# A new order of all pieces in a fused attention and channel-mix kernel: loads of late batches ahead of use, stores and DMA transposes between them

## The chip, the cores and the metric

The kernel runs on one NeuronCore of a Trainium2 chip. The metric is the device time of one execution in microseconds (us). A profile, taken by the hardware profiler, gives a span that is about 2 us shorter than that time.

Names: PE is the tensor engine, DVE the vector engine, ACT the scalar engine, POOL the engine whose queue issues the loads, SP the queue that issues stores and DMA transposes. A wait of an engine is idle time before an instruction, named by what ended it.

## The reference

Inputs q, k, v are [8 batches, 8 heads, 576, 64] in float32. Linear attention with an RMS norm is followed by a channel mix with weights 512x1024 (w_k), 1024x512 (w_v) and 512x512 (w_r):

```python
def _attn_ref(q, k, v, g_norm):
    kv = np.einsum('bhsd,bhse->bhde', k, v)
    out = np.einsum('bhsd,bhde->bhse', q, kv)
    rms = np.sqrt(np.mean(out * out, axis=-1, keepdims=True) + 1e-06)
    return (out / rms * g_norm).astype(np.float32)

def _moe_ref(x, mu_k, mu_r, w_k, w_v, w_r):
    x_prev = np.concatenate([np.zeros((B, 1, D), dtype=np.float32), x[:, :-1, :]], axis=1)
    xk = mu_k * x + (1.0 - mu_k) * x_prev
    xr = mu_r * x + (1.0 - mu_r) * x_prev
    k = np.maximum(xk @ w_k, 0.0)
    v = k * k @ w_v
    r = 1.0 / (1.0 + np.exp(-(xr @ w_r)))
    return (r * v).astype(np.float32)
```

## The kernel before

The kernel is a list of named pieces and one long string, ORDER, that gives the order in which they are emitted. Each engine runs its own pieces in that order. A token is `name:engine:slots`; a slot is a buffer of a small set. The pieces that matter here, by batch b and group g of 512 rows:

- `load_k4.0` loads k of batch 4 (float32 in DRAM, written as bf16), on the POOL queue. There are two slots each for k, v and q.
- `kv4.0` multiplies k by v of batch 4 on PE. It is the last reader of their slots.
- `qTd4` transposes q of batch 4 by DMA on the SP queue (batches 3 to 7; batches 0 to 2 are transposed by PE, `qT2.0`). `u4.*` then multiplies by kv.
- `K`, `R`, `V` are the matmuls with w_k, w_r and w_v, `S` the stores on the SP queue.

How the order is run, and a load (cut):

```python
    def run(self, order, idle):
        held = {}
        for token in order.split():
            name, eng, slots = (token.split(":") + ["", ""])[:3]
            if name == "idle":
                idle(int(eng), int(slots))      # matmuls on zeros
                continue
            p = self.pieces[name]
            ...
            for b, s in zip(new, slots):
                old = held.get((b.tag, s))
                assert old is None or all(u.done for u in old.users), name
                b.slot = int(s)
                held[(b.tag, s)] = b
            p.done = True
            p.fn(self.ENG[eng] if eng else next(iter(p.on)))
...
    BUFS = {
        "k": (2, (NP, H, NJ * HD), BF16),
        "v": (2, (NP, H, NJ * HD), BF16),
        "q": (2, (NP, H, NJ * HD), BF16),
        "qT": (2, (128, H, NI * NP), BF16),
        ...
        "out": (4, (128, 2, C), FP32),
        "ps": (4, (128, 2, 512), FP32),
    }
...
    def load(b, n, h0, h1):
        def fn(_):
            nc.gpsimd.dma_start(out=get(kvq[(n, b)])[:, h0:h1, :], in_=rows(n, b, h0, h1))
...
            def q_dma(_):
                nc.sync.dma_start_transpose(out=get(qT).rearrange(...), in_=get(qin).rearrange(...))
...
    def idle(n, slot):
        for _ in range(n):
            nc.tensor.matmul(tiles[("ps", slot)][:, 0, HS:512], zeros[:, 0:128], zeros[:, HS:512], start=True, stop=True)
```

The part of ORDER that decides the loads of batches 3 to 5 (all other tokens cut):

```
kv2.0::2 ... load_q3.0::1 ... load_v3.0::1 ... load_q4.0::0 load_k3.0::1 ... kv3.0::2 ... qTd3::1 ...
load_v5.0::0 load_v4.0::1 ... load_k4.0::0 ... S0.2 qTd4::0 ... load_k5.0::1 ... kv4.0::2 ... load_v6.0::1 ...
kv5.0::0 ... load_k6.0::0 ... S0.1 S0.3 S1.1 ... load_q5.0::1 ... S1.3 ... kv6.0::0 ... S1.0 S0.0 qTd5::1
```

Note that v5 takes slot 0, which kv2 frees, and v4 the slot that kv3 frees. k4 could go out after kv2, but stands behind v5 and v4 in the one POOL queue.

## Time and profile before

| | before |
|---|---|
| median time at the start, 3 runs | 220.16 us (220.15 to 221.36) |
| span of the profiled run | 219.1 us |
| PE busy | 193.7 us (88%) |
| longest wait of PE | 11.0 us, for k of batch 4 |
| last matmul ends, after the start | 213.2 us |

The page first. Each digit is the busy share, in tenths, of one of 40 equal slices of the span (5.5 us each); PEclk is the clock granted to PE in tenths of full speed.

```profile
...
PE   7758999999899009999999999999999999999990
...
PEclk9999999999999956999999999999999999999997
DMA  6999999999999995999999840100004606001184
...
```

PE is full nearly everywhere but in the slices from 71 to 82 us. DMA is full up to about 130 us, and the clock drops just after PE's gap.

Busy time of the engines in stretches of 10 us; the number after the engines is the granted clock, then the share of time that the DMA engines were busy (it sums the time of all packets, so it can pass 1) and what they moved:

```profile
...
core 0: us, PE busy (x) PEld busy (x) DVE busy (x) ACT busy (x) POOL busy (x), PEclk, DMA share, GB/s
...
10.00:20.00 10.00, 6.07 (x71) 3.00 (x70) 9.43 (x26) 8.68 (x15) 5.54 (x9) 1.00 1.27 203
...
70.00:80.00 10.00, 1.06 (x12) 0.24 (x9) 4.11 (x7) 2.58 (x4) 0.00 (x0) 0.80 1.23 253
80.00:90.00 10.00, 7.91 (x72) 3.96 (x72) 1.87 (x4) 3.19 (x3) 3.06 (x4) 0.69 0.81 130
...
```

PE works 1.06 us of 70-80, and at 0.69 of its clock in 80-90.

PE's own timeline there (start, duration, what, and in brackets the idle time before it and what ended that):

```profile
...
70.62 0.44 PE L432 MATMUL ps<-qT,kv 64*64 64x288 bf16 x8
82.09 1.49 PE L349 MATMUL ps<-v,k 96*64 96x64 bf16 x48 [11.03 <-DMA k<-in_k_dram]
83.51 3.23 PE L600 MATMUL ps<-xk,w_k 128*128 128x512 bf16 x8
86.58 3.62 PE L622 MATMUL ps<-w_r,xr 128*128 128x512 bf16 x16
...
```

kv4 (the 48 matmuls with k) waits 11.03 us for k4. The eight w_k matmuls behind it (L600) take 3.23 us, against 1.90 at 68.79 us in the same view.

The loads on POOL, with what each waited for, and the SP queue (an SP row's length is how long issuing kept the queue):

```profile
...
43.07 0.77 POOL L277 DMA_DIRECT2D q<-in_q_dram  x1 [10.07 <-PE ps L407]
43.83 0.77 POOL L277 DMA_DIRECT2D k<-in_k_dram  x1
45.86 0.77 POOL L277 DMA_DIRECT2D v<-in_v_dram  x1 [1.26 <-PE ps L349]
60.05 0.77 POOL L277 DMA_DIRECT2D v<-in_v_dram  x1 [13.42 <-PE ps L349]
60.81 1.58 POOL L277 DMA_DIRECT2D k<-in_k_dram  x2
...
```

```profile
...
47.32 8.04 SPq L390 DMA_TRANSPOSE qT<-q  x1
...
57.27 6.62 SPq L390 DMA_TRANSPOSE qT<-q  x1
63.94 13.38 SPq L582 DMA_DIRECT2D out_dram<-out  x12
```

In ORDER's sequence these are q4, k3, v5, then v4 at 60.05 and k4, k5 at 60.81. Twelve store DMAs follow at 63.94. The time from issue to landing of v4 and k4:

```profile
...
v<-in_v_dram POOLq DMA_DIRECT2D x1, 576.0 KB, 15.6
k<-in_k_dram POOLq DMA_DIRECT2D x1, 576.0 KB, 21.2
...
```

k4 takes 21.2 us, so it lands at 82.0, when PE starts kv4.

### The profile page before, as it was taken

To read this page: it belongs to the slowest core of one execution; us is meant where nothing else is said; L and a number is where in the kernel's file an instruction comes from. 1 tells how busy PE (TensorE), PEld (TensorE's weight loads), DVE (VectorE), ACT (ScalarE), POOL (GpSimd) and SP (SyncE) were. 2 spreads that over 40 slices of the span, in tenths; PEclk is the share of its full clock that TensorE was granted. 3 is DMA by queue.
4 is the path that set the end of the run, shared out by engine and by line. 5 is a ranking of instruction groups with operands and counts; after the bars stand their busy time and mean duration, and the time that the engine had idled before them with its cause. 6 is when DMAs were issued, how large, how long until landed. Compare 5 with 4: busy or idle time off the path is not lost.

```text
span 219.1 us, 3799 instructions
## 1 busy us (share of the span) xinstructions
PE 193.7 (88%) x1526; PEld 94.1 (43%) x1526; DVE 138.9 (63%) x254; ACT 125.1 (57%) x152; POOL 28.8 (13%) x45
## 2 busy tenths in 40 slices
PE   7758999999899009999999999999999999999990
PEld 6424453543443005534444764444444444444450
DVE  1499068975996501688989898829934992422260
ACT  2579674789365301977669778367566444481100
POOL 7954420120030005000400000000000000000000
PEclk9999999999999956999999999999999999999997
DMA  6999999999999995999999840100004606001184
GB/s 151 192 202 206 202 206 204 204 204 195 163 156 98 265 246 63 202 204 150 163 237 188 220 129 3 48 0 3 0 0 114 174 3 193 0 0 48 31 223 131
DMA packets 39301, 29.71 MB, mean 136 GB/s; under 512 B 13548, under 2 KB 34804, under 8 KB 39284
## 3 DMA queue, kind: packets, MB, share of 16 engines
q0 software_dynamic: 21232, 16.48, 50.1%
q1 hardware_dynamic: 17348, 12.03, 26.2%
q10 hardware_dynamic: 704, 0.95, 1.4%
q8 instruction: 12, 0.20, 0.4%
q14 instruction: 5, 0.04, 0.0%
HBM read 33.56 MB, written 9.44 MB: 196 GB/s over the span
## 4 chain that ended last, share of the span: by engine, by line
PE 64%; DMA 21%; DVE 6%; POOL 4%; issue 1%; ACT 1%; DVEq 0%; POOLq 0%
PE ps L656 24%; PE ps L600 22%; DMA k<-in_k_dram 17%; PE ps L622 10%; DMA v<-in_v_dram 5%; PE ps L349 2%; POOL q L277 1%; DVE xT L536 1%; PE ps L432 1%; POOL v L277 1%; PE ps L531 1%; POOL k L277 1%; DVE sqk L607 1%; DVE sq L195 1%; PE ps L515 1%
## 5 line engine op out<-in xcount | busy, mean ns | idle before, releaser
L656 PE MATMUL ps<-w_v,sqk 128*128 128x512 bf16 (+1 forms) x296 | 67.1, 374 | 0.3 <-DMA w_v<-in_moe_w_v_dram 0.3
L600 PE MATMUL ps<-xk,w_k 128*128 128x512 bf16 (+1 forms) x320 | 66.9, 363 | 0.0
L604 ACT ACTIVATE relu<-ps 128x1024 bf16<-128x1024 f32 x36 | 36.4, 1023 | 41.4 <-PE ps L600 37.1
L600 PEld LDWEIGHTS <-w_k 128*128 128x128 bf16 x320 | 30.9, 99 | 32.0 <-issue 2.8
L656 PEld LDWEIGHTS <-sqk 128*128 128x128 bf16 x296 | 27.5, 98 | 32.2 <-issue 1.4
L607 DVE TENSOR_TENSOR sqk<-relu 128x1024 bf16<-128x1024 bf16 x36 | 24.1, 687 | 26.3 <-ACT relu L604 26.2
L622 PE MATMUL ps<-w_r,xr 128*128 128x512 bf16 x144 | 34.4, 379 | 0.1
L660 DVE TENSOR_TENSOR out<-ps,sig 128x1024 f32<-128x1024 f32 (+2 forms) x21 | 22.2, 1068 | 14.2 <-issue 6.8
L627 ACT ACTIVATE sig<-ps 128x1024 bf16<-128x1024 f32 x18 | 18.4, 1022 | 13.1 <-PE ps L622 6.6
L536 DVE TENSOR_TENSOR xT<-uT,ps 128x576 bf16<-128x576 bf16 x28 | 20.0, 750 | 8.0 <-PE ps L531 8.0
L187 ACT ACTIVATE t<-d,mu_sb 128x576 bf16<-128x576 bf16 x29 | 20.7, 767 | 5.9 <-DVE d L557 5.8
L622 PEld LDWEIGHTS <-xr 128*128 128x128 bf16 x144 | 13.5, 98 | 15.9 <-DVE xr L567 0.8
L349 PE MATMUL ps<-v,k 96*64 96x64 bf16 x288 | 6.2, 204 | 11.9 <-DMA k<-in_k_dram 11.8
L181 ACT CAST uT<-ps 128x576 bf16<-128x576 f32 x16 | 9.9, 639 | 6.9 <-PE ps L432 6.5
L277 POOL DMA_DIRECT2D q<-in_q_dram x12 | 8.6, 715 | 36.5 <-DMA qT<-q 17.1
L277 POOL DMA_DIRECT2D v<-in_v_dram x11 | 8.0, 729 | 38.3 <-PE ps L349 36.9
L557 DVE TENSOR_TENSOR d<-xT 128x1152 bf16<-128x1152 bf16 (+1 forms) x18 | 12.5, 692 | 0.6
L183 DVE CAST uT<-ps 128x576 bf16<-128x576 f32 x12 | 8.9, 754 | 5.5 <-PE ps L432 5.4
L567 DVE TENSOR_TENSOR xr<-t,xT 128x1152 bf16<-128x1152 bf16 (+1 forms) x18 | 12.1, 686 | 0.2
L189 DVE TENSOR_SCALAR t<-d,mu_sb 128x576 bf16<-128x576 bf16 x35 | 11.8, 377 | 0.2
L567 DVE TENSOR_TENSOR xk<-t,xT 128x1152 bf16<-128x1152 bf16 (+1 forms) x18 | 11.7, 683 | 0.1
L349 PEld LDWEIGHTS <-k 96*64 96x64 bf16 x288 | 5.6, 120 | 13.7 <-DMA k<-in_k_dram 12.3
(60 smaller groups left out, 127.1 us busy)
## 6 DMA issues: line engine op xcount, KB each, us to landing
out_dram<-out SPq DMA_DIRECT2D x22, 192.0 KB
q<-in_q_dram POOLq DMA_DIRECT2D x6, 576.0 KB, 12.2
k<-in_k_dram POOLq DMA_DIRECT2D x6, 576.0 KB, 15.5
v<-in_v_dram POOLq DMA_DIRECT2D x6, 576.0 KB, 16.2
out_dram<-out SPq DMA_DIRECT2D x22, 128.0 KB
out_dram<-out SPq DMA_DIRECT2D x22, 64.0 KB
w_k<-in_moe_w_k_dram POOLq DMA_DIRECT2D x2, 512.0 KB, 12.7
w_v<-in_moe_w_v_dram POOLq DMA_DIRECT2D x2, 512.0 KB, 15.2
```

Source lines behind the costliest of these rows:

```text
L187: nc.scalar.mul(out=dst, in_=src, mul=by)
L277: nc.gpsimd.dma_start(out=get(kvq[(n, b)])[:, h0:h1, :], in_=rows(n, b, h0, h1))
L349: nc.tensor.matmul(get(pkv)[64 * e:64 * e + 64, 0, HD * i:HD * i + HD], get(kin)[:, h, HD * j:HD * j + HD], get(vin)[:, h, HD * j:HD * j + ...
L536: nc.vector.tensor_tensor(out=get(xT)[:, 2 * i:2 * i + 2, NP + c:NP + c + HS], in0=flat(slice(2 * i, 2 * i + 2))[:, :, c:c + HS], in1=get( ...
L567: nc.vector.tensor_tensor(out=dst[:, hsl, c0:c0 + S], in0=get(t[key])[:, hsl, :], in1=get(xT)[:, hsl, 0:S], op=ALU.add)
L600: nc.tensor.matmul(get(ps)[:, fc % 2, a0:a1], w_k_sb[:, cc, 128 * fc:128 * fc + 128], xk[:, cc, x0:x0 + a1 - a0], start=(cc == 0), stop=(c ...
L604: nc.scalar.activation(out=get(rt), in_=get(ps), func=AF.Relu)
L607: nc.vector.tensor_mul(out=get(sqk)[:, 2 * f2:2 * f2 + 2, :], in0=get(rt), in1=get(rt))
L622: nc.tensor.matmul(get(ps)[:, ci % 2, :], xr[:, cc, c:c + 128], w_r_sb[:, cc, :], start=(cc == 0), stop=(cc == NHP - 1))
L627: nc.scalar.activation(out=get(sg), in_=get(ps), func=AF.Sigmoid)
L656: nc.tensor.matmul(get(ps)[:, ci % 2, cs], get(sqk)[:, fc, 128 * ci:128 * ci + 128], w_v_sb[:, fc, cs], start=(fc == 0), stop=(fc == NFC - 1))
L660: nc.vector.tensor_mul(out=get(ot)[:, xs, cs], in0=get(ps)[:, xs, cs], in1=get(sg)[:, xs, cs])
```

## The change

Its intent: a new sequence of all pieces, with k, v and q of the late batches loaded well ahead of use, and stores and DMA transposes put between the loads. No piece is added, removed or altered; the engine that does a copy or a scaling changes for some. (`land` is a number for the planner that made the order; nothing reads it at run time.) The diff replaces all of ORDER; its core, with cuts:

```diff
 ORDER = """
-    early_k::0 zero cast_k:D:0 g_load sel_load early_v::1 mu_k_load:A mu_r_load:A cast_v:A:0 idle:28:0 kv0.0::0 load_v0.2
-    load_k0.2 load_q0.2::0 kv0.1::1 load_q0.0 load_q0.4 load_v0.4 load_k0.4 load_q0.6 ident qT0.1::2 qTc0.1:A:0 ones kvm0.1::0
+    zero mu_r_load:A early_k::0 mu_k_load:S early_v::1 cast_k:A:0 load_q1.0::0 load_q0.2::1 load_q0.0 load_q0.4 ident idle:28:0
+    qT1.0::0 ident9 cast_v:A:0 kv0.0::1 ones kvm0.0::0 qT0.1::2 qT0.0::3 g_load qTc1.0:A:0 load_k0.4 load_v0.4 load_k0.2
 ... (cut)
-    load_v3.0::1 sig1.0::0 uc2.3:A sq2.1:D load_q4.0::0 load_k3.0::1 K1.0::3 K1.6::0 relu1.1::1 st2::1 rs2::1 sqk1.1::1 K1.1
-    xk2.0 V1.0b tr2.2:D:0 kvc3.0.1:A tr2.0:A o1.1::0 load_v5.0::0 load_v4.0::1 V1.1a V1.1b o1.0::1 load_k4.0::0 K2.6::3 K2.7
-    K2.5::2 K2.4 S0.2 qTd4::0 relu2.3::1 u3.0::0 u3.2::1 uc3.2:A:1 relu2.2::0 load_k5.0::1 K2.2::3 K2.3 u3.1::1 uc3.0:D xr2.2
+    tr1.2:A:1 load_q4.0::1 xk1.2 xk1.0 o0.0::2 tr1.0:A K1.2::0 load_v3.0::1 K1.3 xr1.0 o0.1::3 xr1.2 relu1.1::1 load_k3.0::1
+    relu1.0::0 u2.1::2 K1.4::0 u2.0::3 uc2.0:A uc2.1:D sqk1.1 u2.2::2 sqk1.0 uc2.2:D sq2.1:D:0 sq2.0:A load_k4.0::0 K1.5
+    relu1.2::1 sqk1.2 R1.1::1 V1.1a::3 st2::2 rs2::1 R1.0 sp2.0::02 x2.0.1::0 x2.0.0 V1.0a V1.0b sp2.1::20 load_v4.0::0 x2.1.1
+    x2.1.0 d2.0::0 d2.2 sig1.0::2 S0.1 qTd3::0 load_q5.0::0 tk2.0:D:0 xk2.0 tk2.2:A xk2.2 R1.3::1 R1.2 V1.1b V1.3a::0 V1.2a
+    u3.3::3 sqk2.2 load_v5.0::1 load_k5.0::1 kv4.0::0 uc3.1:A K2.2::1 K2.3 uc3.3:D sq3.0:D:0 sq3.1:D relu2.3::0 st3::3 rs3::0
 ... (cut)
 """
-    p_wr = add("load_w_r", {"POOL": 0.75}, lambda _: load_w(w_r_sb, moe_w_r), land=2.5)
+    p_wr = add("load_w_r", {"POOL": 0.75}, lambda _: load_w(w_r_sb, moe_w_r), land=3.0)
```

v4 now takes slot 0, freed by kv2, and stands with k4 ahead of q5, v5 and k5.

More of the change, by code (lines that the diff above doesn't have):

```diff
@@ L15 @@
 ORDER = """
-    early_k::0 zero cast_k:D:0 g_load sel_load early_v::1 mu_k_load:A mu_r_load:A cast_v:A:0 idle:28:0 kv0.0::0 load_v0.2
-    load_k0.2 load_q0.2::0 kv0.1::1 load_q0.0 load_q0.4 load_v0.4 load_k0.4 load_q0.6 ident qT0.1::2 qTc0.1:A:0 ones kvm0.1::0
-    ident9 mu_mm::3 mu kvm0.0 load_k0.6 load_v0.6 qT0.0::1 u0.1::3 qTc0.0:A sq0.1::0 qT0.2::2 u0.0::0 uc0.1:D:0 ss0.1::1 sq0.0
-    qTc0.2:D uc0.0:D rs0.1::0 load_w_r kv0.2::3 kvm0.2 x0.1::0 ss0.0::2 d0.1::0 load_k1.0::1 load_v1.0::1 rs0.0::1 load_w_k0
@@ L20 @@
-    x0.0 u0.2::0 sq0.2 tk0.1:D:0 qT0.3::1 kv0.3::3 ss0.2::2 uc0.2:A rs0.2::0 d0.0 kvm0.3 load_w_k1 qTc0.3:D tk0.0:A x0.2
-    tr0.0:D:1 xr0.0 d0.2 tr0.1:D xr0.1 u0.3::0 sq0.3 ss0.3::3 uc0.3:A rs0.3::1 x0.3 d0.3 tr0.2:A tk0.2:A tr0.3:A R0.0::12 R0.1
-    load_k1.4 load_v1.4 load_q1.0::1 tk0.3:A xr0.2 kv1.0::0 xk0.0 xk0.1 xr0.3 R0.2 R0.3.1 R0.3.0 sig0.0::0 xk0.2 xk0.3 K0.3::3
-    kvm1.0::1 K0.2 K0.0::0 relu0.1::0 K0.1 relu0.0::1 sqk0.0::0 sqk0.1 load_q1.4 K0.6::1 K0.4::3 K0.5 K0.7 qT1.1::0 load_w_v0
@@ L24 @@
-    qTc1.1:D:1 sig0.1::1 relu0.2::1 kv1.2::2 qT1.0::3 qT1.3::0 relu0.3::0 qTc1.0:A qT1.2::1 kvm1.2 u1.1::2 uc1.1:A:1 qTc1.3:D
-    u1.0::3 u1.3::0 sel qTc1.2:D u1.2::1 V0.1a::2 uc1.0:D sq1.0:D:0 uc1.3:A uc1.2:A sq1.1:D st1::3 rs1::0 load_w_v1 sqk0.2
-    sqk0.3 load_q2.0::0 V0.0a sp1.1::01 load_k2.0::0 V0.1b x1.1.0::1 x1.1.1 sp1.0::30 x1.0.1 V0.0b V0.3a::1 x1.0.0 d1.2::0
-    qT2.3::0 qTc2.3:A:0 d1.0 tr1.0:D:1 xr1.0 tr1.2:A load_v2.0::0 xr1.2 qT2.2::3 V0.2a V0.3b qT2.1::0 qTc2.2:A qTc2.1:A V0.2b
@@ L28 @@
-    qT2.0::3 tk1.0:A:0 R1.2::0 R1.3 tk1.2:D o0.0::2 qTc2.0:D o0.1::3 xk1.0 xk1.2 kv2.0::2 sig1.1::2 R1.1::3 R1.0 load_q3.0::1
-    kvc2.0.2:A:0 kvc2.0.0:A kvc2.0.1:A u2.1::1 u2.2::0 uc2.2:A:0 uc2.1:D K1.3::2 u2.3::1 u2.0::0 uc2.0:D sq2.0:D:0 K1.2
-    load_v3.0::1 sig1.0::0 uc2.3:A sq2.1:D load_q4.0::0 load_k3.0::1 K1.0::3 K1.6::0 relu1.1::1 st2::1 rs2::1 sqk1.1::1 K1.1
-    relu1.0::0 K1.7 sqk1.0 relu1.3::1 K1.5::2 sp2.1::13 K1.4 x2.1.1::0 x2.1.0 sqk1.3 relu1.2::0 V1.2a::0 V1.3a sp2.0::31
-    kv3.0::2 sqk1.2 qTd3::1 x2.0.1 d2.2::0 x2.0.0 d2.0 tk2.2:A:1 kvc3.0.0:A:1 kvc3.0.2:A V1.2b V1.0a::1 V1.3b tk2.0:D xk2.2
@@ L33 @@
-    xk2.0 V1.0b tr2.2:D:0 kvc3.0.1:A tr2.0:A o1.1::0 load_v5.0::0 load_v4.0::1 V1.1a V1.1b o1.0::1 load_k4.0::0 K2.6::3 K2.7
-    K2.5::2 K2.4 S0.2 qTd4::0 relu2.3::1 u3.0::0 u3.2::1 uc3.2:A:1 relu2.2::0 load_k5.0::1 K2.2::3 K2.3 u3.1::1 uc3.0:D xr2.2
-    xr2.0 u3.3::0 kv4.0::2 uc3.1:A load_v6.0::1 K2.0::1 K2.1 sqk2.3::0 sqk2.2 uc3.3:A relu2.1::1 sq3.1:D:0 sq3.0:D relu2.0::0
-    R2.1::0 R2.0 sig2.0::1 R2.3::3 R2.2 sig2.1::2 sqk2.1 kvc4.0.2:D:0 kvc4.0.1:D sqk2.0 kvc4.0.0:D u4.3::1 uc4.3:D:0 u4.0::2
@@ L37 @@
-    kv5.0::0 kvc5.0.2:D:1 uc4.0:D st3::1 rs3::0 load_k6.0::0 V2.3a::3 V2.3b S0.1 S0.3 S1.1 sp3.0::21 kvc5.0.0:D kvc5.0.1:A
-    u4.2::0 x3.0.1::1 x3.0.0 V2.2a load_q5.0::1 uc4.2:A sq4.1:A:0 sp3.1::10 x3.1.0 V2.2b u4.1::2 x3.1.1 uc4.1:A S1.3 sq4.0:A
-    d3.0::0 V2.1a::1 V2.1b V2.0a tk3.0:A:1 d3.2 tk3.2:D xk3.2 load_q6.0::0 xk3.0 kv6.0::0 st4::2 S1.0 S0.0 qTd5::1 rs4::1 V2.0b
-    o2.0::3 tr3.0:A:0 kvc6.0.1:A:0 kvc6.0.2:D K3.5::2 K3.4 K3.7::1 K3.6 qTd6::0 o2.1::1 S2.0 S1.2 S2.2 load_q7.0::1 load_v7.0::0
@@ L41 @@
-    load_k7.0::1 relu3.2::1 kvc6.0.0:A sqk3.2::1 xr3.0 tr3.2:D xr3.2 relu3.3::0 sqk3.3 K3.1::2 K3.0 K3.2::3 K3.3 sp4.0::01
-    relu3.0::1 sqk3.0 x4.0.0::0 relu3.1::0 sqk3.1 x4.0.1 R3.0::2 R3.1 R3.2::0 sp4.1::31 x4.1.0 x4.1.1 d4.0::0 d4.2 R3.3
-    sig3.0::0 V3.0a::2 V3.0b sig3.1::1 u5.3::3 u5.1::1 u6.0::0 uc5.3:A:1 V3.1a uc6.0:A:0 uc5.1:D tk4.0:D:1 u5.2::3 u5.0::1
-    u6.1::0 V3.1b uc5.0:A sq5.0:A:0 uc5.2:D xk4.0 o3.0::2 tk4.2:D uc6.1:A sq5.1:A V3.2a::1 V3.2b V3.3a xk4.2 u6.2::3 u6.3::0
-    st5::2 uc6.2:D tr4.0:A:0 uc6.3:D rs5::0 V3.3b K4.2::3 K4.3 relu4.1::1 K4.7::0 K4.6 xr4.0 sp5.0::23 tr4.2:D o3.1::0 xr4.2
@@ L46 @@
-    qTd7::1 x5.0.1::1 S2.1 S3.0 x5.0.0 K4.0::1 K4.1 sp5.1::32 relu4.3::0 sqk4.3::0 x5.1.0 sqk4.1 K4.4::0 K4.5 relu4.0::0
-    sq6.1:A:0 relu4.2::1 x5.1.1 d5.2::0 sq6.0:D tk5.2:D:1 sqk4.0 R4.1::3 R4.0 R4.3::1 st6::2 kv7.0::0 R4.2 S3.1 S3.2 S2.3
-    tr5.2:A:0 rs6::1 xk5.2 d5.0 sqk4.2 tk5.0:D kvc7.0.2:D:1 kvc7.0.0:D xk5.0 sig4.1::2 kvc7.0.1:A sig4.0::0 V4.0a::2 V4.1a V4.1b
-    u7.3::1 u7.1::0 u7.2::3 V4.0b uc7.1:D:1 uc7.3:D K5.7::0 uc7.2:A o4.0::3 xr5.2 tr5.0:D xr5.0 K5.1::3 K5.6 relu5.3::0 K5.0
@@ L50 @@
-    relu5.0::1 sqk5.0::1 sqk5.3 K5.2::1 K5.3 K5.5::2 relu5.1::1 K5.4 R5.0::0 R5.1 sp6.0::31 relu5.2::0 sig5.0::1 x6.0.1::0
-    x6.0.0 sqk5.1 V4.2a::2 V4.3a sp6.1::10 u7.0::3 uc7.0:A sq7.1:A:0 sq7.0:A sqk5.2 x6.1.0 x6.1.1 d6.0::0 d6.2 tk6.0:A:1
-    tr6.2:A:0 V4.3b V5.3a::3 V5.1a::1 V4.2b V5.1b R5.3::0 V5.3b R5.2 V5.0a S3.3 tk6.2:D o4.1::2 xk6.2 xk6.0 sig5.1::0 K6.3::2
-    K6.2 V5.0b K6.7::0 K6.6 V5.2a V5.2b relu6.1::1 relu6.3::0 tr6.0:D xr6.2 xr6.0 sqk6.1::0 K6.0::2 sqk6.3 o5.1::1 o5.0::0 K6.1
@@ L54 @@
-    st7::0 K6.5::3 K6.4 rs7::0 relu6.0::1 R6.2::1 R6.3 sp7.1::02 relu6.2::0 sig6.1::2 sqk6.0 x7.1.0::1 x7.1.1 R6.0::3 R6.1
-    sp7.0::01 sqk6.2 x7.0.0 x7.0.1 d7.0::0 d7.2 S4.1 tk7.2:D:1 tk7.0:D tr7.0:A:0 sig6.0::0 V6.0a::2 V6.0b V6.3a::0 V6.1a V6.2a
-    V6.3b V6.1b xk7.2 S5.0 S5.2 S4.0 S5.1 V6.2b xk7.0 o6.0::3 K7.4::1 K7.5 K7.7::3 tr7.2:A o6.1::0 K8.4::2 K8.0::0 relu7.2::1
-    xr7.0 K8.1 relu8.0::0 sqk8.0::1 xr7.2 sqk7.2::0 S5.3 S4.2 S6.2 S6.0 S4.3 S6.1 K7.3::1 K7.2 K8.6::0 relu7.1::0 K8.7
-    relu8.3::1 sqk8.3 K8.5 relu8.2::1 sqk8.2 K7.6 sqk7.1 R8.3::1 K8.3::0 K8.2 relu8.1::1 relu7.3::0 sqk7.3 R8.2 K7.1::2
@@ L59 @@
-    sig8.1::1 sqk8.1 K7.0 relu7.0::0 R8.0::0 R8.1 sig8.0::0 V8.1a::3 V8.1b o8.0.1.0::1 sqk7.0 R7.3::1 R7.2 R7.0::2 sig7.1::2
-    V7.0a::0 V7.3a::3 V7.2a V7.3b V7.0b V7.2b o7.1::2 R7.1 V7.1a V7.1b S7.2 S7.3 S8.1.1.0:A S6.3 sig7.0::2 V8.0a::1 V8.0b
-    V8.2a::3 o7.0::3 S7.0 S7.1 o8.0.0.0 S8.0.0.0:S V8.2b o8.1.2.0::2 S8.2.2.0:A V8.3.0a::2 V8.3.0b V8.3.1a::0 o8.1.3.0
-    S8.3.3.0:S V8.3.1b o8.1.3.1 S8.3.3.1:A
+    zero mu_r_load:A early_k::0 mu_k_load:S early_v::1 cast_k:A:0 load_q1.0::0 load_q0.2::1 load_q0.0 load_q0.4 ident idle:28:0
@@ new lines @@
+    qT1.0::0 ident9 cast_v:A:0 kv0.0::1 ones kvm0.0::0 qT0.1::2 qT0.0::3 g_load qTc1.0:A:0 load_k0.4 load_v0.4 load_k0.2
+    qTc0.0:A:1 load_v0.2 qT0.2::1 mu_mm::0 u0.0::3 qTc0.2:A kv0.2::1 sq0.0::0 mu kvm0.2 qTc0.1:D ss0.0::0 uc0.0:D:0 rs0.0::0
+    load_q0.6 load_v0.6 load_k0.6 u0.2::1 kv0.1::2 kvm0.1 x0.0::0 d0.0::0 sq0.2 ss0.2::0 sel_load uc0.2:A qT0.3::3 u0.1::2
+    rs0.2::1 x0.2 qTc0.3:D d0.2 sq0.1 kv0.3::1 ss0.1::0 load_w_r uc0.1:A rs0.1::0 sel kvm0.3 qT1.1::3 tr0.2:A:0 u0.3::2 tr0.0:D
@@ new lines @@
+    load_v1.0::1 load_k1.0::1 x0.1 sq0.3 ss0.3::1 d0.1 xr0.2 xr0.0 uc0.3:A rs0.3::1 tr0.1:D xr0.1 R0.0::02 R0.1 x0.3 tk0.2:D:1
+    d0.3 qTc1.1:D tr0.3:D xr0.3 R0.2 R0.3.1 load_w_k0 kv1.0::1 tk0.3:A tk0.0:A tk0.1:D xk0.3 xk0.0 xk0.2 xk0.1 R0.3.0 load_w_k1
+    kvm1.0::1 K0.3::3 K0.2 K0.0::1 sig0.0::0 sig0.1::1 relu0.1::0 K0.4::0 u1.1::2 uc1.1:D:1 sqk0.1::0 K0.5 load_q1.4 load_v1.4
+    load_k1.4 relu0.2::1 K0.1 relu0.0::0 sqk0.0 u1.0::3 qT1.3::2 qT1.2::0 uc1.0:A sq1.0:A:0 kv1.2::1 K0.6::3 qTc1.2:D qTc1.3:D
@@ new lines @@
+    kvm1.2 u1.3::0 sqk0.2 u1.2::2 uc1.2:A load_q2.0::1 K0.7 load_w_v0 load_w_v1 load_v2.0::0 load_k2.0::0 load_q3.0::0 qT2.1::1
+    qT2.0::2 uc1.3:D sq1.1:D st1::0 qTc2.1:D:1 qTc2.0:D qT2.2::1 rs1::0 relu0.3::0 sp1.1::20 qTc2.2:D V0.3a::1 V0.1a::3
+    x1.1.1::1 x1.1.0 sqk0.3 sp1.0::02 x1.0.1 x1.0.0 V0.2a V0.0a d1.2::0 V0.1b V0.2b V0.0b V0.3b qT2.3::2 tk1.2:A:0 d1.0 tk1.0:D
+    tr1.2:A:1 load_q4.0::1 xk1.2 xk1.0 o0.0::2 tr1.0:A K1.2::0 load_v3.0::1 K1.3 xr1.0 o0.1::3 xr1.2 relu1.1::1 load_k3.0::1
@@ new lines @@
+    K1.7::3 K1.6 relu1.3::0 kv2.0::0 kvc2.0.1:A:0 kvc2.0.0:D K1.0::1 sqk1.3::1 qTc2.3:A K1.1 kvc2.0.2:A u2.3::3 uc2.3:A:0
+    relu1.0::0 u2.1::2 K1.4::0 u2.0::3 uc2.0:A uc2.1:D sqk1.1 u2.2::2 sqk1.0 uc2.2:D sq2.1:D:0 sq2.0:A load_k4.0::0 K1.5
+    relu1.2::1 sqk1.2 R1.1::1 V1.1a::3 st2::2 rs2::1 R1.0 sp2.0::02 x2.0.1::0 x2.0.0 V1.0a V1.0b sp2.1::20 load_v4.0::0 x2.1.1
+    x2.1.0 d2.0::0 d2.2 sig1.0::2 S0.1 qTd3::0 load_q5.0::0 tk2.0:D:0 xk2.0 tk2.2:A xk2.2 R1.3::1 R1.2 V1.1b V1.3a::0 V1.2a
+    V1.3b V1.2b sig1.1::0 tr2.2:A:1 tr2.0:D o1.0::0 qTd4::1 K2.0::2 K2.1 K2.5::1 kv3.0::3 K2.4 relu2.0::0 kvc3.0.0:A:1
@@ new lines @@
+    kvc3.0.1:A kvc3.0.2:A relu2.2::1 K2.7::2 xr2.0 sqk2.0::0 o1.1::1 xr2.2 u3.0::3 u3.2::0 uc3.2:D:1 uc3.0:A K2.6 u3.1::1
+    u3.3::3 sqk2.2 load_v5.0::1 load_k5.0::1 kv4.0::0 uc3.1:A K2.2::1 K2.3 uc3.3:D sq3.0:D:0 sq3.1:D relu2.3::0 st3::3 rs3::0
+    kvc4.0.0:D:0 kvc4.0.2:D kvc4.0.1:D R2.0::2 relu2.1::1 sp3.0::03 load_q6.0::1 sqk2.3 R2.1 R2.3::1 x3.0.1::1 x3.0.0 sqk2.1
+    sig2.0::1 sp3.1::30 S1.0 x3.1.0 R2.2 sig2.1::2 x3.1.1 d3.0::0 d3.2 S0.0 tk3.2:D:0 xk3.2 u4.3::2 V2.1a::3 V2.1b V2.0a
+    load_v6.0::0 load_k6.0::0 S1.1 S1.3 uc4.3:A:0 tk3.0:A u4.0::0 u4.2::1 u4.1::2 V2.0b uc4.1:A uc4.0:A tr3.0:D:1 xk3.0 o2.0::2
@@ new lines @@
+    V2.3a::2 V2.2a V2.3b V2.2b sq4.0:D:0 tr3.2:D uc4.2:A sq4.1:A st4::0 rs4::1 K3.2::1 sp4.1::30 K3.3 xr3.0 S1.2 qTd5::0 o2.1::0
+    K3.5::2 x4.1.0::0 x4.1.1 sp4.0::30 K3.4 relu3.1::0 xr3.2 x4.0.1 d4.2::0 x4.0.0 d4.0 relu3.2::1 tr4.0:A:0 tk4.0:D:1 sqk3.2::1
+    R3.0::1 K3.7::0 K3.6 R3.2::2 R3.3 R3.1 K3.1::3 K3.0 relu3.3::1 sig3.0::0 tk4.2:D xk4.0 sqk3.3 xk4.2 relu3.0::1 sqk3.0
+    K4.1::0 K4.5::1 K4.0 K4.4 tr4.2:A sig3.1::1 xr4.0 relu4.0::1 sqk3.1 sqk4.0::0 relu4.2::0 load_q7.0::0 K4.3::3 K4.2 kv5.0::2
@@ new lines @@
+    kvc5.0.1:D:1 kvc5.0.0:D kvc5.0.2:D load_k7.0::1 sqk4.2 load_v7.0::1 V3.2a::0 V3.2b relu4.1::1 u5.3::1 u5.2::3 uc5.3:D:1
+    sqk4.1 uc5.2:A sq5.1:A:0 K4.6::2 u5.1::1 u5.0::3 V3.3a V3.3b K4.7 uc5.1:D uc5.0:A sq5.0:D st5::1 rs5::0 S2.3 S0.2 S2.2
+    qTd6::1 S0.3 relu4.3::0 o3.1::1 V3.1a::3 sp5.0::01 xr4.2 x5.0.1::1 x5.0.0 V3.0a V3.1b sp5.1::21 sqk4.3 x5.1.1 kv6.0::0
+    kvc6.0.2:D:0 x5.1.0 d5.0::0 d5.2 tk5.0:D:1 V3.0b R4.3::1 kvc6.0.0:A kvc6.0.1:A V4.0a::2 R4.1::0 R4.2 sig4.1::2 V4.1a R4.0
@@ new lines @@
+    sig4.0::1 u6.1::1 tk5.2:D o3.0::0 xk5.2 xk5.0 uc6.1:D:0 V4.1b u6.0::3 u6.2::0 u6.3::1 uc6.0:A uc6.2:A sq6.0:A:0 V4.0b S3.2
+    S3.0 qTd7::0 S3.3 K5.5::3 K5.4 tr5.0:D:0 xr5.0 uc6.3:D sq6.1:D o4.0::3 tr5.2:D S3.1 relu5.2::1 S2.1 K5.2::0 K5.1::1 st6::2
+    rs6::1 K5.0 V4.3a::3 K5.3 relu5.0::0 sp6.0::21 V4.2a sqk5.2::1 xr5.2 sqk5.0 x6.0.1::0 x6.0.0 relu5.1::1 sqk5.1 V4.3b
+    sp6.1::10 kv7.0::2 V4.2b kvc7.0.0:A:1 x6.1.1 K5.7::0 K5.6 x6.1.0 kvc7.0.2:A kvc7.0.1:D d6.2::0 R5.2::1 R5.3 sig5.1::0
@@ new lines @@
+    R5.1::2 R5.0 relu5.3::0 sig5.0::1 tk6.2:D:1 d6.0 tk6.0:D xk6.0 xk6.2 o4.1::1 K6.1::1 K6.0 tr6.2:D:0 relu6.0::1 K6.5::0
+    K6.3::3 u7.2::2 u7.1::1 tr6.0:D xr6.0 sqk5.3 uc7.1:A:1 K6.2 K6.4 relu6.1::0 V5.3a::1 V5.3b sqk6.1::0 uc7.2:D xr6.2 u7.3::3
+    u7.0::2 uc7.3:D sq7.1:D:0 relu6.2::0 V5.2a V5.2b o5.1::0 R6.2::0 uc7.0:A sq7.0:A st7::2 rs7::0 R6.3 sig6.1::2 R6.0::3 R6.1
+    sig6.0::0 K6.7::1 sqk6.2 sqk6.0 sp7.1::20 K6.6 x7.1.1::1 x7.1.0 relu6.3::0 V6.3a::3 sp7.0::02 V6.2a x7.0.0 sqk6.3 d7.0::0
@@ new lines @@
+    x7.0.1 d7.2 V6.0a::1 V5.1a::0 V6.0b V6.2b V5.1b V6.1a tk7.0:A:1 V5.0a S2.0 S4.0 tk7.2:D tr7.0:D:0 V6.3b xk7.2 xk7.0 o6.1::2
+    V5.0b K8.5::2 K7.7::3 K7.6 V6.1b relu7.3::1 K8.4 relu8.2::0 tr7.2:A S4.3 S4.2 S4.1 o5.0::1 xr7.0 sqk8.2::1 o6.0::3 K8.7::0
+    K8.6 K7.1::3 K7.5::2 relu8.3::0 sqk8.3 sqk7.3::0 xr7.2 K8.2::1 K8.3 relu8.1::0 K8.0::0 K7.0 relu7.0::1 sqk7.0 sqk8.1 K7.4
+    R8.1::1 S6.1 R8.0 relu7.2::1 sqk7.2 R7.3::3 K8.1 relu8.0::0 K7.2::2 R7.2 R7.1::0 K7.3 sig8.0::2 relu7.1::1 R7.0 sig7.0::1
@@ L63 @@
+    sig7.1::0 sqk8.0 V8.0a::1 V8.1a::2 V8.0b S5.3 S5.0 S5.2 S6.0 sqk7.1 o8.0.0.0::0 V7.1a::0 V8.1b o8.0.1.0 V7.3a::3 S5.1 V7.3b
+    V7.1b V7.2a V7.2b o7.1::3 S8.0.0.0:S S8.1.1.0:S V7.0a V7.0b V8.2a::1 R8.2::2 R8.3 V8.2b o7.0::1 V8.3.0a::3 V8.3.0b
+    V8.3.1a::0 V8.3.1b sig8.1::2 o8.1.2.0::0 S7.3 S6.2 o8.1.3.0 S8.3.3.0:A o8.1.3.1 S8.3.3.1:A S6.3 S7.1 S7.0 S7.2 S8.2.2.0:S
 """
```

## The prediction

> **What bounds the kernel now.** The table by stage shows the tensor engine (PE) 88% busy: about 193.7 us in a span of 219.1. The waits of PE sum to some 19 us, and one is far the largest: 11.0 us (71.0 to 82.1) on the landing of k of batch 4. In the table of 10-us stretches PE is busy 1.06 us of 70-80, while the DMA engines are full (share 1.23) from 0 to 130 us. So the first 80 us are bound by the order in which data arrive, the rest by PE, whose necessary work, summed piece by piece at the trace's durations, is 188.6 us in both kernels.
>
> How the stall arises (timeline of the POOL and SP queues): the loads are issued in order by POOL. The load of q4 waits 10.1 us for PE's transposes of q2 and holds k3 behind it until 43.8; k3 lands at 58.8; kv3 then runs and frees the buffers, so v4 and k4 are issued only at 60-61, after q4 and v5, and share the DMA engines with two DMA transposes (8.0 and 6.6 us of issue) and 12 stores (63.9 to 77.3). k4 takes 21.2 us from issue to landing. After it PE is slow: eight w_k matmuls take 3.17 us instead of 1.73, kv4 1.49 instead of 0.97, granted clock 0.69 in 80-90. "TensorE: Matmul & The Clock Gate" of the Trainium skill (Part 1) says that an idle window of about 3.4 us halves the PE clock until it was busy as long; this trace agrees. Cost of the stall: 11.0 + about 2 = 13 us.
>
> **What the change does.** No work is removed. k and v of batch 4 go out as soon as kv2 has freed their slots (estimated 48 us, not 60), right behind q4, v3, k3 and ahead of q5, v5, k5; only one store and the two transposes compete there. Bytes through v4 exceed those through k3 in the old order by two tensors (1.18 MB as written), 5.8 us at the 204 GB/s of the table; with one more transpose some 3 us: landing estimated at 66-69. PE reaches kv4 at 60.8 us of its own work plus 10 to 12 us of bubbles: 71-73. So the stall goes, with 2 to 6 us to spare. Later loads have over 10 us to spare.
>
> What it costs: half of q1 is loaded before k and v of batch 0, and q2 before w_v, so the first w_k matmul starts 1 to 1.5 us later (before: 22.2) and the first w_v matmuls wait more; but transposes of q1 and q2 are done in the meantime: net loss 0.5 to 1.5 us. VectorE gets some more copies and in the stretch of batches 3 and 4 has more work than PE (about 24 us per 20 of PE): 0.5 to 2 us of bubbles. The tail (5.9 us after the last matmul) holds two more stores behind each other on SP: 0 to 1 us more.
>
> **Sum.** PE's end 188.6 + 11.5 + 2 = 202; tail 6.5: span 208.5; measured time is about 1 us over the span: 209.5. Range 206 to 215.5. Faster by over 2%: 0.88; within 2%: 0.10; slower: 0.02.
>
> **To be seen.** No PE wait over 3 us after 10 us; k4 landing before 72; granted clock near 1.0 in all of 20-200; PE idle in 70-90 under 2 us; w_k starting at 23-24; PE busy about 191.5; the chain of waits led by PE.
>
> **What would make it wrong.** DMA transposes slowing the loads more than I reckon (k4 after 73, the stall returning in small); a new wait in the first 40 us for w_k, w_v or k1.4 of more than 2 us; VectorE setting the pace at 60-90; stores piled up at the end.

## The result, and the profile after

| | before | after |
|---|---|---|
| median time, 4 runs each | 220.76 us (220.15 to 221.86) | 211.02 us (209.39 to 211.81) |
| ratio | | 0.9544 (0.9466 to 0.9622) |
| span of the profiled run | 219.1 us | 207.6 us |
| PE busy | 193.7 us | 195.7 us |
| granted clock over the span | 0.969 | 0.971 |

A ratio here is the mean time of one kernel's runs over the mean of the other's runs of the same rounds, so it is not quite the ratio of the medians quoted. Executions over 1.5% slower than the fastest of the same kernel are left out of the means. The profiled run of after is its fastest.

The page after, and the stretches that answer to those of before:

```profile
...
PE   7598999999999999999999999999999999999970
...
PEclk9955999999999999999999999999999999999998
...
```

```profile
...
10.00:20.00 10.00, 8.71 (x80) 4.13 (x80) 7.33 (x22) 8.06 (x13) 6.75 (x10) 0.56 1.28 201
...
70.00:80.00 10.00, 10.00 (x116) 4.19 (x116) 9.19 (x17) 8.60 (x10) 2.90 (x4) 1.00 1.23 267
80.00:90.00 10.00, 10.00 (x66) 4.15 (x64) 9.62 (x17) 7.32 (x11) 0.00 (x0) 1.00 1.32 178
...
```

PE is busy throughout 70-90, at full clock (so it is in every such stretch from 40 to 200). In this profile the clock is 0.56 in 10-20, where the profiled run before had 1.00. A drop there is not peculiar to the new order: the profiles of a1, a2 and a3 below, which keep the old start, show 0.83 in 10-20.

PE at kv4, the loads on POOL, the SP queue, and the landing of k4 and v4:

```profile
...
71.48 0.44 PE L431 MATMUL ps<-qT,kv 64*64 64x288 bf16 x8
71.85 0.95 PE L348 MATMUL ps<-v,k 96*64 96x64 bf16 x48
...
```

```profile
...
44.86 0.77 POOL L276 DMA_DIRECT2D q<-in_q_dram  x1 [12.58 <-PE ps L406]
45.62 0.77 POOL L276 DMA_DIRECT2D v<-in_v_dram  x1
46.38 0.77 POOL L276 DMA_DIRECT2D k<-in_k_dram  x1
49.20 0.77 POOL L276 DMA_DIRECT2D k<-in_k_dram  x1 [2.05 <-PE ps L348]
49.96 0.77 POOL L276 DMA_DIRECT2D v<-in_v_dram  x1
67.22 0.77 POOL L276 DMA_DIRECT2D q<-in_q_dram  x1 [16.50 <-DMA qT<-q]
...
```

```profile
...
46.84 21.61 SPq L389 DMA_TRANSPOSE qT<-q  x2
68.55 7.59 SPq L581 DMA_DIRECT2D out_dram<-out  x10
...
```

```profile
...
k<-in_k_dram POOLq DMA_DIRECT2D x1, 576.0 KB, 17.2
v<-in_v_dram POOLq DMA_DIRECT2D x1, 576.0 KB, 20.2
...
```

k4 is issued at 49.20 and lands at 66.4; v4 is issued at 49.96 and lands at 70.2. PE reaches kv4 at 71.85 and does not wait. So 1.7 us were to spare. The two transposes kept the SP queue for 21.61 us and the twelve stores did not come between.

PE's longest waits by kind (total, times, longest), the first of before and the two first of after:

```profile
...
PE ps L349 <- DMA k<-in_k_dram: 11.8, 2, 11.0
...
```

```profile
...
PE ps L401 <- DMA q<-in_q_dram: 2.1, 3, 1.5
PE ps L702 <- DVE zeros L227: 1.2, 1, 1.2
...
```

The sum of the difference, from the two timelines and spans: PE comes to kv4 at 71.85 instead of 71.06 (+0.8); the wait of 11.0 is gone (-11.0); from kv4 to the last matmul 129.1 us instead of 131.1 (-2.0, nearly all of it the time after the gap at half clock: kv4 1.49 against 0.95 us, the eight w_k matmuls behind it 3.23 against 1.90); from the last matmul to the end 6.6 instead of 5.9 us (+0.7). Together -11.5, which is the difference of the spans. The medians differ by less, 9.7, mainly since the profiled run of after is its fastest: the spans of its other timed runs are 208.6 to 210.0.

### The profile page after: what moved, and what is told of

Read it like the earlier page. It is cut to its first block, busy times and chain, and to the rows that moved or that the text cites. A ratio compares the mean times of both kernels' runs of the same rounds, so it can differ in the third digit from the quotient of the medians.

```text
span 207.6 us, 3798 instructions
## 1 busy us (share of the span) xinstructions
PE 195.7 (94%) x1526; PEld 93.9 (45%) x1526; DVE 141.1 (68%) x262; ACT 122.0 (59%) x146; POOL 28.7 (14%) x45
## 4 chain that ended last, share of the span: by engine, by line
PE 88%; DMA 3%; ACT 2%; POOL 2%; DVE 1%; issue 1%; POOLq 0%
PE ps L655 31%; PE ps L599 30%; PE ps L621 16%; DMA v<-in_v_dram 3%; PE ps L348 3%; PE ps L431 2%; PE ps L363 2%; PE ps L530 2%; POOL q L276 1%; PE ps L514 1%; PE ps L425 1%; PE ps L476 1%; ACT relu L603 1%; ACT L200 1%; DVE xr L566 0%
## 5 line engine op out<-in xcount | busy, mean ns | idle before, releaser
L599 PE MATMUL ps<-xk,w_k 128*128 128x512 bf16 (+1 forms) x320 | 67.4, 358 | 0.0
L599 PEld LDWEIGHTS <-w_k 128*128 128x128 bf16 x320 | 30.1, 98 | 29.9 <-issue 1.6
L606 DVE TENSOR_TENSOR sqk<-relu 128x1024 bf16<-128x1024 bf16 x36 | 24.5, 687 | 21.2 <-ACT relu L603 21.1
L621 PE MATMUL ps<-w_r,xr 128*128 128x512 bf16 x144 | 35.5, 389 | 0.1
L659 DVE TENSOR_TENSOR out<-ps,sig 128x1024 f32<-128x1024 f32 (+2 forms) x21 | 22.3, 1069 | 11.5 <-PE ps L655 9.0
L186 ACT ACTIVATE t<-d,mu_sb 128x576 bf16<-128x576 bf16 x23 | 16.4, 767 | 13.1 <-DVE d L556 13.1
L188 DVE TENSOR_SCALAR t<-d,mu_sb 128x576 bf16<-128x576 bf16 x41 | 13.5, 372 | 0.2
L556 DVE TENSOR_TENSOR d<-xT 128x1152 bf16<-128x1152 bf16 (+1 forms) x18 | 12.4, 692 | 0.6
L276 POOL DMA_DIRECT2D k<-in_k_dram x11 | 7.9, 715 | 12.8 <-PE ps L348 10.7
```

Source lines behind the costliest of these rows:

```text
L186: nc.scalar.mul(out=dst, in_=src, mul=by)
L188: nc.vector.tensor_scalar_mul(out=dst, in0=src, scalar1=by)
L599: nc.tensor.matmul(get(ps)[:, fc % 2, a0:a1], w_k_sb[:, cc, 128 * fc:128 * fc + 128], xk[:, cc, x0:x0 + a1 - a0], start=(cc == 0), stop=(c ...
L606: nc.vector.tensor_mul(out=get(sqk)[:, 2 * f2:2 * f2 + 2, :], in0=get(rt), in1=get(rt))
L621: nc.tensor.matmul(get(ps)[:, ci % 2, :], xr[:, cc, c:c + 128], w_r_sb[:, cc, :], start=(cc == 0), stop=(cc == NHP - 1))
L659: nc.vector.tensor_mul(out=get(ot)[:, xs, cs], in0=get(ps)[:, xs, cs], in1=get(sg)[:, xs, cs])
```

## The experiments

The theory (A): the 11 us were lost because k and v of batch 4 went out only after kv3. Rivals: (B) PE's new order keeps it fed; (C) stores and transposes in the window held k4 up. A second question is the half clock at the start (theories D, E and F, named in the expectations below). All outputs are right.

### The load order alone: v4 and k4 first (a2_v4k4_first)

The kernel before, with only these tokens changed:

```diff
-load_v5.0::0 load_v4.0::1 V1.1a V1.1b o1.0::1 load_k4.0::0 K2.6::3
+load_v4.0::0 load_k4.0::0 load_v5.0::1 V1.1a V1.1b o1.0::1 K2.6::3
-load_v6.0::1
+load_v6.0::0
-load_v7.0::0
+load_v7.0::1
```

> The kernel before, with nothing changed but the POOL queue: v4 takes the slot that kv2 frees and goes out with k4 at 45 to 47 us, v5 takes the later slot. Theory A (the time was lost because k and v of batch 4 were issued only after kv3): k4 and v4 land by 66 to 69, the 11.0 us wait of PE at kv4 falls under 1.5 us and the clock stays at 1.0 through 70-90. Rival B (the load order is not enough by itself; the new order of PE's work, with kv5 and kv6 25 us of PE work later, is what keeps PE fed): a new wait appears at kv5 or kv6, 3 to 6 us in all, and the time is 212 to 216 instead of 207 to 209. Rival C (what held k4 were the 12 stores and two transposes): the stall shrinks by less than half, time 215 to 220.

Measured: 211.16 us median (before 220.24), ratio 0.9595 (0.952 to 0.9671). v4 is issued at 46.07 and k4 at 46.84; k4 lands 20.3 us later, at 67.1.

```profile
...
PE ps L349 <- DMA k<-in_k_dram: 2.1, 2, 1.5
...
```

```profile
...
71.08 0.95 PE L349 MATMUL ps<-v,k 96*64 96x64 bf16 x48
...
87.84 0.95 PE L349 MATMUL ps<-v,k 96*64 96x64 bf16 x48 [1.49 <-DMA k<-in_k_dram]
...
```

kv4 starts at 71.08 without a wait, and the clock stays at 1.00 in 60-100. A new wait of 1.49 us appears at kv6, for k6 (87.84), as rival B said in kind; the rest of the 2.1 us is 0.66 before kv3, which was there already. A few tokens give most of the gain of the whole reorder; B is worth about 1.5 us, not 3 to 6. The edit had one effect more than its tokens show: the second transpose kept the SP queue until 70.15, so the twelve stores began at 70.20, after k4 had landed. It removed both the late issue and the stores beside k4; the run with the late stores below separates the two.

### The same, and k3 ahead of q4 (a1_k3_too)

```diff
-load_q4.0::0 load_k3.0::1
+load_k3.0::1 load_q4.0::0
```

> As the run with v4 and k4 first, and k3 is issued ahead of q4, that is at about 33 us instead of 43.8. My prediction named the wait of q4's load, which holds k3, as the start of the stall. If that matters, this run is faster than the one without it by over 1 us, with kv3 no longer waiting (0.7 us before) and v4, k4 landing earlier. If only the issue of v4 and k4 matters, the two are within 1 us of each other. k3 should land at 50 to 54 instead of 58.8.

Measured: 210.62 us, ratio 0.9552 (0.9487 to 0.9616), which is not told apart from 0.9595. k3 was issued at 33.43 and landed 19.8 us later at 53.2, and kv3 no longer waited, but k4 landed at 66.9, as before this edit. This was tested on top of the mended order; but in the kernel before, too, kv3 waited only 0.74 us for k3, so the load of q4 can have put off v4 and k4 by no more than that. It was not what made the stall.

### The stores moved out of the window (a3_stores_late)

The kernel before with its loads as they were:

```diff
-S0.1 S0.3 S1.1 ... S1.3 ... S1.0 S0.0 qTd5::1
+... qTd5::1 S0.1 S0.3 S1.1 S1.3 S1.0 S0.0
```

> The kernel before, its loads as they were, but the 12 stores of 64 to 77 us moved behind the transpose of q5, so that they run after 97 us. Theory A: v4 and k4 are still issued at 60-61, two transposes still run before; k4 lands at 75 to 79 and 4 to 8 us of the 11.0 us stall stay. Rival C (the stores are the cause): the stall falls under 2 us. Some PE wait near 100 us may appear because the output buffers come free later; it is not counted.

Measured: one look, 224.82 us. k4, issued at 60.7 as before, landed 14.6 us later instead of 21.2.

```profile
...
75.36 1.49 PE L349 MATMUL ps<-v,k 96*64 96x64 bf16 x48 [4.41 <-DMA k<-in_k_dram]
76.79 3.59 PE L600 MATMUL ps<-xk,w_k 128*128 128x512 bf16 x8
...
```

```profile
...
PE ps L600 <- DVE out L660: 6.7, 2, 4.0
...
```

Of the wait 4.41 us stay. So, by one profile each, the stores held k4 up by some 6.7 us (82.0 to 75.3); they were an accomplice, and late issue alone still costs 4.4 us. The time is no gain: PE then waits 6.7 us for output buffers that come free late, and the clock drops a second time there (0.83 in 100-110). This one run took 4.6 us more than the median before; I have not accounted for all of it. The Trainium skill, "DMA: Bandwidth & Descriptors", section "Issuing engines are not separate DMA queues", says that DMAs of all issuing engines run on the same 16 engines and interleave; this pair of runs agrees, stores of the SP queue delaying a load of the POOL queue by 6.7 us.

### One part of the change undone (a4_undo)

The changed kernel with v5 in the slot that kv2 frees, v4 and k4 after kv3:

```diff
-load_k4.0::0 K1.5 ... load_v4.0::0 x2.1.1 ... load_q5.0::0 ... load_v5.0::1 load_k5.0::1 kv4.0::0
+load_v5.0::0 K1.5 ... x2.1.1 ... load_v4.0::1 load_k4.0::0 load_k5.0::1 load_q5.0::0 kv4.0::0
-load_v6.0::0
+load_v6.0::1
-load_v7.0::1
+load_v7.0::0
```

> The changed kernel with one part undone: v5 takes the slot that kv2 frees, v4 and k4 go out only after kv3 (about 68.5 us), followed by k5 and q5. Theory A: v4 and k4 land at 75 to 79, PE waits 4 to 7 us at kv4 (reached at 71.9)[...]; time 4 to 9 us over the changed kernel's 211.0, so 215 to 220. Rival B (the new PE order absorbs late loads): under 1.5 us of wait and a time within 2 us of the changed kernel.

Measured: 223.82 us (223.3 to 224.47), beyond what I expected, and 1.0168 (1.0112 to 1.0224) of before.

```profile
...
83.05 1.49 PE L348 MATMUL ps<-v,k 96*64 96x64 bf16 x48 [9.77 <-DMA k<-in_k_dram]
84.47 3.59 PE L599 MATMUL ps<-xk,w_k 128*128 128x512 bf16 x8
...
```

The stall is back, with 9.77 us; k4 is issued at 70.8 and lands 12.2 us later, at 83.0. I had reckoned with the two loads alone; ten stores ran beside them from 68.1 to 74.5 us, and the experiment with the late stores shows what such stores cost. The rest is clock: eight w_k matmuls (L599) take 3.59 us. Rival B is refuted: the new order of PE does not absorb a late k4.

### The half clock at the start: control (after_again)

The profiles of the changed kernel and of its undo both had a clock near 0.5 in 10-20 (0.56 and 0.52). For the next three experiments the changed kernel ran again, unaltered, as control on the same chip.

> The changed kernel itself, as the control for the three runs beside it on the same chip: 209.5 to 212, granted clock 0.5 to 0.6 in 10-20 in its profile, first w_k matmul at 24.5 to 25.5 us.

Measured: 211.20 us (210.83 to 211.75), ratio 0.9637 (0.9592 to 0.9681); the first w_k matmul started at 26.99 us, later than expected.

### More idle matmuls before the first q (w1_idle44)

```diff
-idle:28:0 qT1.0::0
+idle:44:0 qT1.0::0
```

> The changed kernel with 44 instead of 28 idle matmuls at the start, so that PE is busy until the first q has landed at 7.2 us. Theory D (the half clock of 11 to 21 us is caused by the idle 1.5 us before the first transpose): the clock stays 1.0 in 10-20, the first w_k matmul starts at 22.5 to 23.5 instead of 24.9, time 1.5 to 2.5 us under the control. Rival E (it is the thin work of 7 to 12 us, where PE does small matmuls with gaps): the clock in 10-20 stays at 0.5 to 0.6 and the time within 0.7 us of the control. Rival F (the data and the other engines set the start of w_k, not the clock): the clock rises, the time stays within 0.7 us.

Measured: 210.06 us (208.95 to 212.07), ratio 0.9595 (0.9535 to 0.9656). In the profiled run the clock was full up to 16 us and fell then, 0.58 in 16-20 and 0.57 in 20-24; w_k started at 25.73. The six timed runs have mean clocks from 0.958 to 0.994, so in at least one (0.994, 209.10 us) the drop hardly came. Neither D nor E as I had put them: the idle time before the first transpose was one of several places where the clock could fall.

### Idle matmuls in six further gaps (w3_fill_all, w3_again)

```diff
-qT0.1::2 qT0.0::3 ... qT0.2::1 ... kv0.2::1 ... u0.3::2 ... ss0.3::1 ... R0.3.1
+qT0.1::2 idle:3:0 qT0.0::3 ... idle:3:0 qT0.2::1 ... idle:4:0 kv0.2::1 ... idle:6:2 u0.3::2 ... idle:4:1 ss0.3::1 ... idle:4:1 R0.3.1
```

> As the run with 44 idle matmuls, and 3 to 6 more idle matmuls in each of six gaps up to 20 us. Theory D: as that run, within 0.5 us. Rival E: the clock is 1.0 here and not there, and the time is 1.5 to 2.5 us under the control. Rival F: clock 1.0, time within 0.7 us of the control.

> The changed kernel with 44 and 22 idle matmuls, run again beside the next one: 208.5 to 209.5, spread under 1.5 us, clock over 0.99.

Measured: 209.02 us (208.77 to 209.89), ratio 0.954 (0.9495 to 0.9585), beside the control's 211.20; on another chip 209.15 (208.94 to 209.69), ratio 0.9498. The stretches of the control first, then of this kernel (w3_again):

```profile
...
10.00:20.00 10.00, 9.26 (x90) 4.96 (x90) 6.35 (x20) 7.98 (x13) 6.45 (x10) 0.50 1.29 202
20.00:30.00 10.00, 9.63 (x53) 4.12 (x55) 5.53 (x16) 6.34 (x8) 3.15 (x5) 0.75 1.28 205
...
```

```profile
...
10.00:20.00 10.00, 8.28 (x117) 5.32 (x111) 7.03 (x22) 8.80 (x15) 6.37 (x9) 1.00 1.28 194
20.00:30.00 10.00, 9.74 (x69) 4.73 (x67) 6.22 (x16) 6.11 (x8) 3.07 (x4) 1.00 1.28 204
...
```

The clock is 0.989 to 0.998 over the span in all twelve runs. So the half clock at the start cost the changed kernel about 2.2 us. The spread is 1.1 and 0.8 us, against 3.1 with the first gap alone filled; but the control's was 0.9 too, and c1_fill below spreads over 2.4 us at clocks of 0.988 to 0.994. That the clock makes the spread is not shown. w_k starts at 24.8 to 25.1; in one of the two profiles it waits 0.21 us for the landing of w_k.

### Old start, mended loads, filled gaps (c1_fill)

The kernel of a1_k3_too with 33 idle matmuls first and 3 to 10 more in five gaps up to 20 us:

```diff
+idle:33:0 kv0.0 ... idle:3:0 kv0.1 ... idle:3:1 u0.2 ... idle:10:0 u0.3 ... idle:5:3 ss0.3 ... idle:5:0 kv1.0
```

> The kernel before with its load order mended (v4, k4 first, k3 ahead of q4; that run took 210.6) and with idle matmuls in six gaps of its start. In that run the clock was 0.83 in 10-20. If the start is bound by the clock: clock 1.0, time 1 to 2 us under 210.6 and less spread among its runs. If by data and the other engines: within 0.7 us of 210.6, as most of its start is waits of PE.

Measured: 209.75 us (208.8 to 211.19), ratio 0.957 (0.952 to 0.9621). The clock rose from 0.83 in 10-20 to 1.00, but the ratio is not told apart from that of the run without fillers (0.9552, on another chip), and w_k starts at 22.69 us against 22.25 there. In this order the start waits for data and other engines; the clock costs nothing that these ratios show.

### And kv6 later (c2_fill_kv6)

```diff
-xk3.0 kv6.0::0 st4::2 ... tr3.0:A:0 kvc6.0.1:A:0 kvc6.0.2:D K3.5::2 K3.4 K3.7::1
+xk3.0 st4::2 ... tr3.0:A:0 K3.5::2 K3.4 kv6.0::0 kvc6.0.1:A:0 kvc6.0.2:D K3.7::1
```

> The kernel before with its load order mended, its start filled, and kv6 put six pieces later in PE's order (4.2 us of PE work), since k6 landed 1.6 us too late for it. If that wait was lost time: it goes, and the time is 1 to 2 us under the 209.75 of the run without it, so 207.8 to 208.8, equal to or under the changed kernel with filled gaps. If another wait takes its place (VectorE at 90-105): within 0.7 us of 209.75.

Measured: 208.47 us (207.98 to 208.97), ratio 0.9462 (0.9404 to 0.9519), beside 209.15 (208.94 to 209.69) of w3_again on the same chip.

```profile
...
PE ps L703 <- DVE zeros L228: 1.2, 1, 1.2
PE ps L432 <- DMA qT<-q: 0.6, 2, 0.4
...
```

No wait for k is left; after the first 1.2 us, in which PE waits for the zeros, the longest kind is 0.6 us in all. This is the fastest kernel, by medians 0.7 us under the filled new order (a small lead: the intervals of the two ratios, 0.9404 to 0.9519 and 0.9448 to 0.9549, overlap): the order before, with its loads mended, its start filled and one piece moved.

## Why the prediction was right, point by point

- **The bound, and the stall.** Right, and the clock as the Trainium skill has it ("TensorE: Matmul & The Clock Gate", Part 1). The 11.0 us wait went, and with it the half clock behind it (0.50 from 76.0 to 86.2 us): 2.0 us from kv4 to the last matmul. I had said 11.0 + about 2. The undo brings a stall of 9.8 us back, and the load order alone removes it.
- **How the stall arose.** Partly wrong. I began the chain with the load of q4, which waits 10.1 us and holds k3. In the changed kernel q4's load waits even longer (12.58 us in the lines above) and k3, issued at 46.4 and 15.8 us on the way, lands at 62.2, later than before; and putting k3 ahead of q4 left the landing of k4 where it was. The step that counts is the next one of my text: v4 and k4 behind kv3 and v5.
- **The stores.** I named them among what competed, without a size. They were worth 6.7 us of k4's landing.
- **Landing of k4 and v4: 66 to 69, 2 to 6 us to spare.** k4 at 66.4, v4 at 70.2, 1.7 us to spare. What was off is where the sum starts, not the time for the bytes. I counted from k3's old landing at 58.8; but q4's load waited 12.58 us, until 44.86 (before: 43.07), v3 now stands between it and k3, and so k3 was issued 2.6 us later than before (46.38, not 43.83) and landed at 62.2. The DMA engines meanwhile moved only 29 to 90 GB/s in 45-48 (before: 201 to 205). From k3's landing to v4's it took 8.0 us, against the 5.8 + 3 that I had reckoned. The two transposes kept the SP queue for 21.6 us, where I knew durations of 8.0 and 6.6, and the load of q5 had to wait for them until 67.2; what they cost k4 and v4 no run separates.
- **Start: w_k at 23 to 24, net loss 0.5 to 1.5 us.** w_k started at 24.8 in the fastest run and at 27.0 in the control. By the time PE reached kv4 the loss had shrunk to 0.8 us in the profiled run, but what I did not foresee is the half clock from 11 to 21 us. By estimate it is also why PE is busy for 195.7 us and not 191.5: some 9 us of its busy time lie in that stretch at half clock, and full clock would have saved half of them. Filling the gaps brought 2.2 us.
- **VectorE bubbles of 0.5 to 2 us at 60-90.** None: PE is busy 10.00 of each 10 us from 40 to 200.
- **Tail 6.5 us.** 6.6.
- **The sum.** 209.5 against 211.0: span 208.5 against 207.6 in the fastest run, but I added 1 us from span to time where it is 1.7 to 2.2. The missing bubbles and the half clock had opposite signs, so the sum is better than its terms; that was luck.
- **Chances.** Faster by over 2% was given 0.88; the interval of the ratio, 0.9466 to 0.9622, lies wholly there.

What stays open: which condition exactly drops the clock at the start. It varies among runs of one kernel, and the runs show only that filling the gaps prevents it. The same thin stretch can go either way: in 14-16 PE was busy 0.43 us in the profile of before and 0.42 us in that of a1, which have the same start; the first kept the full clock, the second ran at half clock from about 15.7 to 19 us.

## What to carry to other kernels

When one engine waits for a load, look first at when the load was issued and what stood before it in its queue and its slot; here five tokens gave nearly all that the new order of the whole kernel gave. An in-order load queue with two slots should hold its loads in the order of their use, with the next batch in the first slot that comes free. And after a reorder look at the clock of the start: a start of small matmuls with gaps can lose part of what the order has won (here about 2.2 of some 10 us, in the other order nothing measurable).

## What the Trainium skill lacked or had wrong

- "TensorE: Matmul & The Clock Gate", Part 1, gives the half clock as coming after an idle window of about 3.4 us. The long gaps agree roughly: in the kernel before the clock was 0.50 from 76.0 us on, 4.9 us after the last matmul (71.06), and full again from 86.2; with the late stores it fell 2.5 us after the last matmul (70.96 to 73.4), in the undo 2.0 us after it (73.28 to 75.2). But Part 1 gives no amount of work that still counts as idle. If the window is 3.4 us long, the undo's held some 1.4 us of work, an estimate from that figure. In the changed kernel PE idled at most 1.54 us at a stretch before the drop, was busy 0.84 us of 6-8 and 1.41 us of 8-10 by the profile, and still ran at 0.50 from 12 to 20 us. Of its matmuls from 7 to 10 us 48 were transposes by PE; whether these count no run here separates.
- The same page, in its paragraph on the warm-up budget, puts the ramp penalty under 1% of a typical span and calls it run-variable. Both are about right here: 2.2 of 211.2 us (1.0%; control against filled gaps), nothing measurable in another order of the same work (0.957 against 0.9552), and mean clocks from 0.958 to 0.994 in six runs of one kernel (w1_idle44). The paragraph is about the first warm-up; here the loss comes from drops after it.
- "DMA: Bandwidth & Descriptors", section "Latency and other measured facts", gives an effective bandwidth for DMA transposes, 261 GB/s with a non-contiguous mid-dim. No page says how long one of this size keeps its issuing queue (the page's cycle counts of issue are for other tile counts): here the same 576 KB took the SP queue 3.0 to 12.4 us, the 3.0 with no loads beside it (at 121.85 us), and delayed the next stores and the load that reuses the buffer.
- The same page's Specifications give an HBM limit of about 358 GB/s per core. That line alone misleads for a kernel on one core; the page's own section "Bandwidth" says so, where a core whose neighbour is idle gets more. Loads in this kernel, on one core, ran at 204 GB/s as written in bf16 for long stretches; each 2-byte element was read as 4 bytes, so an estimate from that is 408 GB/s read.
